# Preparing the next block unit behind the second of seven products, in a fused RWKV-6 attention and SiLU MLP kernel

## The chip, the cores and the metric

The kernel runs on one core of a Trainium2 chip. The metric is the device time of that core in microseconds (us), the median over several runs. A core has five engines with queues of their own, each in order: TensorE (PE in the profile; its weight loads are PEld), VectorE (DVE), ScalarE (ACT), GpSimd (POOL) and SyncE (SP), which here issues nearly all DMAs. Matmuls write to an accumulator memory, PSUM; VectorE and ScalarE read it out.

## The reference

Two stages in float32. First an RWKV-6 attention: for each of 4 batches and 8 heads a 48 x 48 state is carried over 768 tokens.

```python
for t in range(S):
    kt, vt, rt, wt = (k[:, :, t], v[:, :, t], r[:, :, t], w[:, :, t])
    cur = np.einsum('bhd,bhe->bhde', u[None] * kt, vt)
    y[:, :, t] = np.einsum('bhd,bhde->bhe', rt, state + cur)
    state = wt[:, :, :, None] * state + np.einsum('bhd,bhe->bhde', kt, vt)
```

Then the result, as 3072 tokens of 384 channels, goes through an MLP with 2048 hidden channels:

```python
h = x @ w_in
g = h * (1.0 / (1.0 + np.exp(-h)))
return (g @ w_out).astype(np.float32)
```

## The kernel before

**Units.** The tokens are cut into 12 units: six blocks of 128 tokens (`L`) by two pairs of batches. A unit is 256 token columns for the MLP. The first units have a special treatment; from unit 4 (`NPAIR`) on a unit is a "block unit", whose bonus terms (the part with u, and the products inside blocks of 8 tokens) are computed on GpSimd and VectorE.

**Attention of a unit.** The loaded r, k and w (`raw`) are transposed on VectorE (L374) to channels by tokens: `tr`, `tk`, `tw`. `product` (L422) multiplies neighbouring columns of the decays w on GpSimd, level by level, so that level l holds products over 2^l tokens. `grow_keys` (L645) and `grow_own` (L654) multiply the keys with these products on GpSimd; `grow_queries` (L627) does it to the queries on VectorE. `burst` (L704) makes the scores of two levels on TensorE, and `keep_level` (L722) puts them in the score matrix under a mask. `block_bonus` (L507) makes elementwise products of r, k and w in eight steps on GpSimd; `block_sum` (L541) adds them up on VectorE into `block_sums`, which goes out to memory and back by `block_move` (L560, L563). Step 4 of `block_bonus` overwrites `ruk`, which step 0 of `block_sum` reads. At the end of a unit `y_state` (L844) and `y_values` (L852) give the output, ScalarE copies it to `yt` (L857), `update` (L879, L884, L893) makes the new state, and `move_x` (L915) issues ten DMAs on SP that lay `yt` out as `xt`, the input of the MLP. `xt` has a single buffer.

**MLP of a unit.** `up` (L987) makes two of 16 tiles of hidden channels, ScalarE applies SiLU (L996), and `sums` (L1035) forms sums of quarters on VectorE. The second matrix product is done in Strassen's manner by seven smaller products: `quarter` (L1053), each 16 matmul instructions into one of two buffers `p_o` in PSUM. What stands in the buffer is drained by additions on VectorE (L1062); the first product is drained by a copy on ScalarE (L1060). Two products complete the output of a batch, and issue its DMA on SP (L1066). In the order of issue products 2, 3 and 4 read the sums (`own`, `temps` in the profile's names).

**Order.** The schedule is written by hand: each engine carries out its instructions in the order in which the program issues them, and waits on semaphores where data or a buffer is needed. The loop over the units from 3 on interleaves the attention of unit i, cut into groups by `mix(i)`, with the steps of the MLP: the seven products of unit i - 2, then the eight `up` steps of unit i - 1. `room` says how many of these steps follow each group; for a block unit it begins with 3, behind an empty group. The last group of `mix(i)` is the third entry of `end`. It ends with the steps that prepare unit i + 1 and with `move_x(i)`.

**Loads.** `loads` is the list of DMAs for r of the next unit and w and k of the next but one, with the values of the next in their middle. It is dealt out over the groups in `behind`, to the end of each group. The last share thus stands behind `move_x(i)` in SP's queue. Each `load_blocks` step is four DMAs (L123).

Of the kernel before, what the change touches and what calls it, by code (L numbers as in the profile page):

```python
# [38 lines left out]
def kernel(  # L39
# [26 lines left out]
    units = [(n, b0) for n in range(S // L) for b0 in range(0, B, NB)]  # L66
    NSLOT = 2
    NTOK = 2
    NPAIR = 4
# [221 lines left out]
    room = pt.tile([128, 4, DM // 2], F32, name="partial", bufs=1).rearrange("p x d -> p (x d)")  # L291
# [179 lines left out]
    at = 768  # L471
# [447 lines left out]
    def both(fn, i, *args):  # L919
        return [(fn, i, b, *args) for b in range(NB)]  # L920

    def block_loads(i, names="wkr"):
        return [(load_blocks, i, name, g) for name in names for g in range(4)]

    def mix(i):

        ahead = i + 1 < len(units)

        def at(now, *steps):
            return steps if now else ()  # L930

        def bonus_steps(j, *steps):
            return [(block_bonus, j, x) for x in steps]

        def sum_steps(j, *steps):
            return [(block_sum, j, x) for x in steps]

        def turns(j):
            return [*both(turn, j, "w"), (product, j, 0), *both(turn, j, "k"), *both(turn, j, "r"), (grow_own, j, 0)]

        def start(j):
            return [*[(product, j, l) for l in range(1, NL)], (grow_own, j, 1)]

        end = [[*at(ahead, *bonus_steps(i + 1, 0, 1, 2, 3))],
               [*at(i < len(units) - NB, (turn_apart, i), (turn_k, i)), *at(ahead, *turns(i + 1))],
               [(y_state, i), *both(y_values, i), *both(update, i), *at(ahead, *start(i + 1)),
                *at(ahead, *sum_steps(i + 1, 0, 1), *bonus_steps(i + 1, 4, 5)), (move_x, i)]]
        if i < NPAIR:
            groups = [[*both(turn, i, "w"), (product, i, 0)],
                      [*both(turn, i, "k"), *both(turn, i, "r"), (odd_ones, i)], [(start_levels, i), (prepare_keys, i, 1)],  # L950
                      [(prepare, i, 1), *[(product, i, l) for l in range(1, NL)]],
                      [(burst, i, 1), (keep_level, i, 1)],
                      [(keep_level, i, 2), (go_on, i, 2)],
                      [(prepare, i, 3), (reverse_v, i), (bonus, i, 0)],
                      [(burst, i, 3), (keep_level, i, 3), (bonus_sum, i, 0), (bonus, i, 1), (bonus, i, 2)],
                      [(keep_level, i, 4), (go_on, i, 4), (bonus_sum, i, 1), (load_rk, i + 1), (load_u,)],
                      [(prepare, i, 5), (make_block_mask,), (bonus_spread, i), (bonus_write, i)],
                      [(burst, i, 5), (keep_level, i, 5), (keep_level, i, 6), (go_on, i, 6)], *end]
        else:
            groups = [[], [(odd_keys, i, 2), (grow_keys, i, 2, False), (grow_queries, i, 2), *sum_steps(i, 2)],  # L960
                      [(prepare, i, 3), *bonus_steps(i, 6, 7)],
                      [(burst, i, 3), (keep_level, i, 3), *sum_steps(i, 3, 4), (block_move, i), *at(ahead, (load_rk, i + 1))],
                      [(keep_level, i, 4), (go_on, i, 4)],
                      [(prepare, i, 5), (reverse_v, i)],
                      [(block_spread, i), (block_write, i)],
                      [(burst, i, 5), (keep_level, i, 5), (keep_level, i, 6), (go_on, i, 6)], *end]

        loads = [*at(i >= NPAIR and ahead, *block_loads(i + 1, "r")), *at(i + NSLOT < len(units), *block_loads(i + NSLOT, "wk"))]
        if i + 1 < len(units):
            loads.insert(len(loads) // 2, (load_values, i + 1))  # L970

        behind = groups[10 if i < NPAIR else 4 if i == NPAIR else 1:][:4 if i + NSLOT >= len(units) else None]
        for at, group in enumerate(behind):
            group += loads[at * len(loads) // len(behind):(at + 1) * len(loads) // len(behind)]
        return groups
# [92 lines left out]
    def ups(i):  # L1068

        steps = [[(up, i, m)] for m in range(FC // 2)]  # L1070
        for m in range(FH // 2 - 1):

            steps[FH // 2 + 1 + m].append((sums, i, m))
        steps[-1].append((sums, i, FH // 2 - 1))
        return steps

    def downs(i):
        return [[(quarter, i, x)] for x in range(7)]

    def do(*steps):  # L1080
        for fn, *args in steps:
            fn(*args)
# [69 lines left out]
    for i in range(3, len(units)):  # L1152
        steps = downs(i - 2) + ups(i - 1)
        groups = mix(i)
        if i == NTOK + 1:
            groups[4].insert(1, (weight_sums, 3))
        room = (1, 1, 0, 2, 1, 1, 1, 1, 1, 2, 2, 1, 1, 0) if i < NPAIR else (3, 2, 2, 1, 1, 1, 2, 1, 1, 1, 0)
        for group, count in zip(groups, room):
            do(*group)
            for step in steps[:count]:  # L1160
                do(*step)
            steps = steps[count:]
# [32 lines left out]
```

## Time and profile before

| | us |
|---|---|
| median of 3 runs | 606.24 (606.04 to 606.5) |
| the profiled execution | 607.39 |
| its span, first to last instruction | 605.6 |
| seven products (L1053), TensorE busy | 210.1 |
| up (L987), TensorE busy | 259.0 |
| drains of the products (L1062), VectorE busy | 27.4 |

The granted clock of TensorE is 1.0 throughout. The products' time is the sum of four groups of the profile, which names them by what they read: 88.7 + 87.4 + 30.4 + 3.6. The drains' is 11.8 + 7.9 + 7.7. Most of the kernel is a steady loop: from about 130 us on the same series of stages comes back each 45 to 47 us, once for each unit. In the timelines a row is start, duration, engine, line, operation, what it writes and reads, and how many instructions were merged in it; square brackets name the idle time before it and what ended it. SPq is SP's queue, whose durations are those of issuing a DMA and not of the transfer.

### The profile page before, as it was taken

Reading aid. Unit: us, or ns where it says so; the run is one execution under the profiler, and the core shown is the slowest. Engines: PE = TensorE matmul, PEld = TensorE weight load, DVE = VectorE, ACT = ScalarE, POOL = GpSimd, SP = SyncE. Lnnn points to the kernel's source line nnn. Section 1 sums busy time; section 2 is a strip of 40 time slices with the busy share of each in tenths; the row PEclk is TensorE's granted clock in tenths of the full one; section 3 lists DMA queues with packets and bytes.
Section 4 is the critical chain, followed back from the end, with each engine's and each line's share of the span. In section 5 each row is a group of like instructions: output and inputs, shape, how many; then the busy total and the mean of one; then the engine's idle time right before and its main releaser. Section 6 shows DMA issues by size and latency. Waiting matters only on the chain.

```text
span 605.6 us, 15147 instructions
## 1 busy us (share of the span) xinstructions
PE 593.4 (98%) x5982; PEld 529.5 (87%) x5982; DVE 416.8 (69%) x709; ACT 233.2 (39%) x516; POOL 366.6 (61%) x414
## 2 busy tenths in 40 slices
PE   8999999999998999999999999999999999999997
PEld 7787876799888899888889889889889989989997
DVE  7879779798795695696696687587587587451041
ACT  6788874431520530440351351351252242241110
POOL 6998777357578578378478478478568558500000
PEclk9999999999999999999999999999999999999999
DMA  9966693343532543643642643543553441100000
GB/s 224 312 148 168 124 307 47 56 77 49 127 70 48 106 65 52 137 61 56 130 65 50 130 62 53 121 69 52 115 83 53 98 70 27 36 2 27 28 1 26
DMA packets 203079, 53.44 MB, mean 88 GB/s; under 512 B 186752, under 2 KB 194816, under 8 KB 203008
## 3 DMA queue, kind: packets, MB, share of 16 engines
q1 hardware_dynamic: 201424, 51.88, 42.0%
q8 instruction: 47, 0.77, 0.6%
q10 hardware_dynamic: 1584, 0.59, 0.5%
q14 instruction: 24, 0.20, 0.1%
HBM read 43.21 MB, written 5.24 MB: 80 GB/s over the span
## 4 chain that ended last, share of the span: by engine, by line
PE 75%; DVE 8%; DMA 5%; POOL 3%; ACT 3%; SPq 2%; issue 2%; DVEq 0%; POOLq 0%; ACTq 0%
PE p_h L987 31%; PE p_o L1053 31%; PE p_m L1009 3%; PE p_m L852 2%; PE p_sc L704 2%; DMA tokens_w<-in_w_dram 2%; POOL tk L645 2%; DVE temps L1035 2%; PE p_m L704 1%; SPq L123 1%; PE p_m L844 1%; DVE score L722 1%; DVE tr L627 1%; DMA u_bc<-in_u_dram 1%; DVE p_w L242 1%
## 5 line engine op out<-in xcount | busy, mean ns | idle before, releaser
L987 PE MATMUL p_h<-xt,w_in_sb 128*128 128x256 f32 x1152 | 259.0, 382 | 0.9 <-POOL tk L669 0.7
L987 PEld LDWEIGHTS p_h<-xt,w_in_sb 128*128 128x128 f32 x1152 | 215.8, 190 | 32.1 <-POOL tk L669 0.9
L996 ACT ACTIVATE gt<-p_h 128x512 f32<-128x512 f32 x90 | 53.6, 597 | 189.4 <-PE p_h L987 189.1
L645 POOL TENSOR_TENSOR tk<-tk,tw 128x256 f32<-128x256 f32 x128 | 91.2, 734 | 42.8 <-issue 22.9
L1053 PE MATMUL p_o<-own,temps 128*128 128x192 f32 x528 | 88.7, 327 | 3.8 <-DVE temps L1062 3.8
L1053 PEld LDWEIGHTS p_o<-own,temps 128*128 128x128 f32 x528 | 86.0, 190 | 4.7 <-DVE temps L1062 4.6
L1053 PE MATMUL p_o<-w_out_sb,gt 128*128 128x192 f32 x508 | 87.4, 328 | 0.0
L1053 PEld LDWEIGHTS p_o<-w_out_sb,gt 128*128 128x128 f32 x508 | 82.7, 190 | 0.9 <-issue 0.4
L507 POOL TENSOR_TENSOR ruk<-tokens_rk 128x768 f32<-128x768 f32 (+1 forms) x32 | 51.3, 1613 | 49.6 <-DMA tokens_rk<-in_k_dram 25.5
L1035 DVE TENSOR_TENSOR temps<-gt 128x256 f32<-128x256 f32 x84 | 55.8, 664 | 22.4 <-ACT gt L996 22.4
L627 DVE TENSOR_TENSOR tr<-tr,tw 128x512 f32<-128x512 f32 x61 | 56.4, 925 | 18.2 <-PE p_m L704 14.4
L422 POOL TENSOR_TENSOR tw<-tw 128x256 f32<-128x256 f32 (+6 forms) x83 | 43.1, 519 | 37.1 <-DVE tw L374 33.2
L615 ACT COPY tk<-tk 128x256 f32<-128x256 f32 x52 | 21.0, 404 | 97.0 <-POOL tk L645 70.1
L1062 DVE TENSOR_TENSOR partial<-p_o,partial 128x192 f32<-128x192 f32 x33 | 11.8, 358 | 38.3 <-PE p_o L1053 38.1
L722 DVE COPY_PREDICATED score<-mask,p_sc 128x512 f32<-128x512 int8 x42 | 31.2, 798 | 3.1 <-PE p_sc L704 2.9
L1035 DVE TENSOR_TENSOR temps<-temps,gt 128x256 f32<-128x256 f32 x43 | 32.2, 748 | 1.5
L1053 PE MATMUL p_o<-w_out_sb,temps 128*128 128x192 f32 x176 | 30.4, 326 | 0.0
L1062 DVE TENSOR_TENSOR temps<-p_o,partial 128x192 f32<-128x192 f32 x22 | 7.9, 357 | 32.7 <-PE p_o L1053 23.3
L507 POOL TENSOR_TENSOR spare<-tokens_rk 128x384 f32<-128x384 f32 (+1 forms) x16 | 29.3, 1833 | 0.0
L857 ACT COPY yt<-p_m 48x512 f32<-48x512 f32 x40 | 23.2, 581 | 14.9 <-PE p_m L852 10.1
L1053 PEld LDWEIGHTS p_o<-w_out_sb,temps 128*128 128x128 f32 x176 | 28.9, 190 | 0.0
L704 PEld LDWEIGHTS p_sc<-tr,tk 48*32 48x32 f32 (+1 forms) x1312 | 18.2, 119 | 11.3 <-issue 6.8
(187 smaller groups left out, 840.5 us busy)
## 6 DMA issues: line engine op xcount, KB each, us to landing
w_out_sb<-in_moe_w_in_dram SPq DMA_DIRECT2D x6, 768.0 KB, 7.4
w_out_sb<-in_moe_w_out_dram SPq DMA_DIRECT2D x4, 768.0 KB, 5.8
own<-in_moe_w_out_dram SPq DMA_DIRECT2D x4, 768.0 KB, 6.2
tokens_rk<-in_r_dram SPq DMA_DIRECT2D x8, 384.0 KB, 4.4
tokens_rk<-in_k_dram SPq DMA_DIRECT2D x8, 384.0 KB, 5.4
tokens_w<-in_w_dram SPq DMA_DIRECT2D x8, 384.0 KB, 6.4
xt<-yt SPq DMA_DIRECT2D x60, 48.0 KB, 2.0
raw<-in_w_dram SPq DMA_DIRECT2D x80, 32.0 KB, 2.0
```

Of the source, the lines that this page charges most:

```text
L422: engine.tensor_tensor(out=up, in0=t[:, :, 0::2], in1=t[:, :, 1::2], op=ALU.mult)
L507: mul = lambda out, one, two: nc.gpsimd.tensor_tensor(out=out, in0=one, in1=two, op=ALU.mult)
L615: nc.scalar.copy(out=keys(i, X[(l + 1) % 2] * L + c, [4 * c, blocks], [c, 2], [1, c]), in_=keys(i, NP * L + c, [4 * c, blocks], [NP * L + ...
L627: nc.vector.tensor_tensor(out=odd, in0=odd, in1=tw[i][l][:, :, 0::2][:, :, :, None].to_broadcast([128, Q, L >> (l + 1), c]), op=ALU.mult)
L645: nc.gpsimd.tensor_tensor(out=out, in0=have, in1=odd_products(i, l, b, *blocks), op=ALU.mult)
L704: nc.tensor.matmul(to, lhsT=tk[i][rows, X[l % 2] + p, x * m:(x + 1) * m], rhs=have, start=True, stop=True)
L722: nc.vector.copy_predicated(out=dst, mask=masks[l][:, :, None].to_broadcast([128, NB, NP, ni, c]), data=sc[e].rearrange("p (b q) (i c) -> ...
L857: nc.scalar.copy(out=yt[i][PD * e:PD * e + D, :, b, :], in_=p_yt[i, e][PD * b:PD * b + D])
L987: nc.tensor.matmul(p_h[:, a, :], lhsT=w_in_sb[:, c, f * 128:(f + 1) * 128], rhs=xt[i][:, c, :], start=(c == 0), stop=(c == KC - 1))
L996: nc.scalar.activation(out=gt[i, m], in_=p_h, func=AF.Silu)
L1035: nc.vector.tensor_tensor(out=out, in0=one, in1=two, op=op)
L1053: nc.tensor.matmul(p, lhsT=left(f), rhs=right[:, f, :], start=(f == 0), stop=(f == FH - 1))
```

## The change

`end` loses the steps that prepare the next unit: `start` (products of levels 1 to 6 on GpSimd; `grow_own` of level 1, which is two multiplications of the keys on GpSimd and one of the queries on VectorE), block sums 0 and 1, and bonus steps 4 and 5. They are issued in the next unit's `mix` instead, as a new second group, and `move_x` of the unit before goes with them. `room` begins with 2 and 1 for 3, so that products 0 and 1 are issued ahead of the new group and product 2 behind it. All other groups keep their place among the steps; the indices of `behind` are raised by one, since a group was put in front. The last share of the loads stays at the end of its group, and so is issued ahead of the moved steps.

```diff
         end = [[*at(ahead, *bonus_steps(i + 1, 0, 1, 2, 3))],
                [*at(i < len(units) - NB, (turn_apart, i), (turn_k, i)), *at(ahead, *turns(i + 1))],
-               [(y_state, i), *both(y_values, i), *both(update, i), *at(ahead, *start(i + 1)),
-                *at(ahead, *sum_steps(i + 1, 0, 1), *bonus_steps(i + 1, 4, 5)), (move_x, i)]]
+               [(y_state, i), *both(y_values, i), *both(update, i), *at(not ahead, (move_x, i))]]
...
         else:
-            groups = [[], [(odd_keys, i, 2), (grow_keys, i, 2, False), (grow_queries, i, 2), *sum_steps(i, 2)],
+            groups = [[], [*start(i), *sum_steps(i, 0, 1), *bonus_steps(i, 4, 5), (move_x, i - 1)],
+                      [(odd_keys, i, 2), (grow_keys, i, 2, False), (grow_queries, i, 2), *sum_steps(i, 2)],
                       [(prepare, i, 3), *bonus_steps(i, 6, 7)],
...
-        behind = groups[10 if i < NPAIR else 4 if i == NPAIR else 1:][:4 if i + NSLOT >= len(units) else None]
+        behind = groups[10 if i < NPAIR else 5 if i == NPAIR else 2:][:4 if i + NSLOT >= len(units) else None]
...
-        room = (1, 1, 0, 2, 1, 1, 1, 1, 1, 2, 2, 1, 1, 0) if i < NPAIR else (3, 2, 2, 1, 1, 1, 2, 1, 1, 1, 0)
+        room = (1, 1, 0, 2, 1, 1, 1, 1, 1, 2, 2, 1, 1, 0) if i < NPAIR else (2, 1, 2, 2, 1, 1, 1, 2, 1, 1, 1, 0)
```

## The prediction

> **What bounds the kernel now.** I read the busy line of the page first (busy us, share of the span, instructions), then TensorE's waits, then the timeline of each engine around the two longest of them.
>
> ```profile
> PE 593.4 (98%) x5982; PEld 529.5 (87%) x5982; DVE 416.8 (69%) x709; ACT 233.2 (39%) x516; POOL 366.6 (61%) x414
> ```
>
> TensorE's waits (line, tile, who ended the wait; us in total, times, longest):
>
> ```profile
> PE p_o L1053 <- DVE temps L1062: 3.8, 2, 2.4
> PE p_m L1088 <- POOL ident masks.py:199: 1.4, 1, 1.4
> PE p_sc L704 <- DVE score L722: 0.8, 2, 0.6
> ```
>
> TensorE is busy for 593.4 of 605.6 us, so an edit that adds no matmul and takes none away can gain only from the 12.2 us in which TensorE idles. The waits say where: 3.8 us in two waits of the quarter products (L1053) for VectorE's drain of an earlier product (L1062). All other named waits are below 1.5 us and lie in the first 130 us, ahead of the edited loop.
>
> The first of the two, where unit 4 begins (start, duration, engine):
>
> ```profile
> 178.18 2.76 PE L1053 MATMUL p_o<-own,temps 128*128 128x192 f32 x16
> ...
> 183.33 5.47 PE L1053 MATMUL p_o<-own,temps 128*128 128x192 f32 x32 [2.38 <-DVE temps L1062]
> ...
> 179.64 1.12 DVE L893 TENSOR_TENSOR state<-p_sc,state 48x384 f32<-48x384 f32 x2
> 180.77 0.79 DVE L627 TENSOR_TENSOR tr<-tr,tw 128x512 f32<-128x512 f32 x1
> 181.49 0.94 DVE L541 TENSOR_REDUCE block_sums<-ruk 128x16 f32<-128x768 f32 x1
> 182.35 0.54 DVE L541 TENSOR_REDUCE block_sums<-spare 128x8 f32<-128x384 f32 x1
> 182.92 0.36 DVE L1062 TENSOR_TENSOR temps<-p_o,partial 128x192 f32<-128x192 f32 x1
> ...
> 185.03 1.13 DVE L541 TENSOR_REDUCE block_sums<-ruk 128x4 f32<-128x192 f32 x4 [0.90 <-POOL ruk L507]
> ...
> 182.51 2.49 POOL L507 TENSOR_TENSOR ruk<-tokens_rk 128x384 f32<-128x384 f32 x2 [1.49 <-DVE block_sums L541]
> ```
>
> Number the seven products 0 to 6. There are two p_o buffers: product 3 needs the one that product 1 leaves. Product 1 ended at 178.2, its drain came at 182.92, behind the state update and three instructions that prepare unit 4. TensorE finished product 2 at 183.33 - 2.38 = 180.95 and stood still. The second wait is the same at unit 6: product 3 starts at 277.71 after 1.39 us of waiting. At the six other units (5, 7 to 11) VectorE is earlier: at unit 5 the drain starts at 229.09, before product 2 ends at 229.85, and nothing waits.
>
> **The change part by part.** For the eight units 4 to 11:
>
> TensorE and ScalarE keep their orders. So does GpSimd, since products 0 and 1 issue nothing there. Two queues change.
>
> (a) VectorE: the drain of product 1 now stands ahead of the moved L627 and the two L541.
>
> Unit 4: the state update ends at 180.76, the drain runs 180.77 to 181.13. In the trace TensorE went on 0.05 us after the drain's end (183.28 to 183.33), so product 3 starts at 181.18 and not at 183.33: 2.15 us gained, 0.23 of the stall stays.
>
> What is late next: the moved steps, by the drain's 0.36 us. GpSimd's pair that overwrites ruk (L507) waits for the first L541, so it runs 182.87 to 185.36; the four small L541 wait for that pair and end at 186.16 + 0.36 = 186.52; behind them stands the drain of product 3, from 186.60 (it kept 0.08 of distance) to 186.96, and product 5 needs its buffer: 187.01. TensorE would be there at 181.18 + 5.31 = 186.49 (products 3 and 4 took 183.33 to 188.64). A **new wait** of 0.52 us. Product 5 started at 188.64, so unit 4 brings 188.64 - 187.01 = 1.63 us.
>
> Unit 6: the state update ends at 275.12, the drain by 275.5, product 2 at 277.71 - 1.39 = 276.32: the whole 1.39 us goes. Product 5 is due at 276.32 + 5.31 = 281.63; the drain of product 3 (280.62 before) ends at 281.34. No new wait, with 0.24 us to spare.
>
> Units 5, 7 to 11: no wait to gain. VectorE now waits for the end of product 1 before the moved steps: at unit 5 to about 227.35 (a drain starts some 0.15 after its product: 230.00 after 229.85), so L627 comes at 227.71 instead of 226.94, 0.77 us later. What covers it: the drain of product 2 had 0.55 us of idle before it, and two idles of 2.24 us follow. Cost 0; were the cover gone, 6 x 0.77 = 4.6 us.
>
> (b) A rule against row. In the Trainium skill, "GPSIMD Engine Reference", Specifications, says GpSimd shares its SBUF interfaces with VectorE and meets contention from VectorE instructions with two SBUF inputs. The second L627 (tr and tw) is one. The ruk pair took 2.49 us at units 4 and 6, where that L627 ran inside it, and 1.97 at unit 5, where it ran only at the pair's end; rule and row point the same way. They differ in the sum: by the mean row (L507, 1613 ns for mixed shapes) there is nothing to choose, by the rule the order decides. With 1.97 us the new wait at unit 4 would be nil and the gain 2.15. I take 2.49, because L627 still falls inside the pair at unit 4 (183.6 to 184.3). By the same reading the pair becomes 2.49 at the other six, while the tokens_w product behind it returns from 1.04 (unit 5) to 0.59 (unit 4): GpSimd is 0.77 + 0.52 - 0.45 = 0.84 us late there. At unit 5 its keys for the next burst of scores ended at 236.00 and TensorE came for them at 240.29; then GpSimd itself waited 1.23 us for TensorE. Both hold 0.84 us. Cost 0.
>
> (c) SP: the ten issues of move_x fall behind the last chunk of loads of the next unit but one (12 DMAs for unit 4, 8 for units 5 to 10, none for 11). Unit 5 is the tight one, since SP is behind there:
>
> ```profile
> 228.91 7.40 SPq L915 DMA_DIRECT2D xt<-yt  x10
> ...
> 236.34 4.04 SPq L123 DMA_DIRECT2D raw<-in_k_dram  x8
> ...
> 241.38 4.80 PE L987 MATMUL p_h<-xt,w_in_sb 128*128 128x256 f32 x21
> ```
>
> The moves will start 4.04 us later, at 232.95; at the usual 0.588 us each the last starts at 238.25 and lands 1.9 us (the median) later at 240.2. L987 begins at 241.38 and needs the last three pieces only at its third chunk, four matmuls of about 0.22 us on (60 of them take 13.15 us in the chain of waits): 242.25. Slack 2.1 us. In the trace one of these issues took 1.70 us and a landing 3.6: with both the last would land at 239.36 + 3.6 = 242.96, 0.7 us late. I take 0, being nearer to the median; 0 and 0.7 are the ends. Unit 4: moves start at 180.9, landed by 189, needed at 195.0. Unit 6: started at 277.6, landed by 286, needed at 289.4. The other units have SP earlier still. The loads that now come first are for a unit later and gain nothing.
>
> (d) Does the gain of unit 4 live on to unit 6? VectorE's lateness at unit 6 comes through SP: out of the block sums sent out at 245.40, the tokens, and GpSimd's products on them. SP's work at unit 4 was restarted at 197.71 by a VectorE block sum that follows TensorE's burst, so it moves with TensorE's 1.63 us; I take all of it. If it did not move, VectorE would stay on its old clock at unit 6 while TensorE comes 1.63 us earlier: product 5 would start at 281.39 there (behind the drain that ends at 281.34), where it started at 277.71 + 5.31 = 283.02, and all that is left of both gains is 1.63 us.
>
> Sum: 1.63 + 1.39 = 3.02 us. Against the profiled execution: 607.39 - 3.02 = 604.37 (span 605.6 to 602.6). The median of the runs is 606.24, 1.15 below the profiled one; the same stalls taken from it give **603.2**.
>
> **The rivals.**
>
> - Partial gain: (d) fails, or xt is late at unit 5. With (d) failing 1.63 us is left, 604.6; xt alone 3.02 - 0.7 gives 603.9. For it: SP issues without a gap from 202 to 245 in the trace. Against: the restart at 197.71.
> - No change: the wait is replaced by another of its size. The drain of product 3 waits behind GpSimd's pair, and at unit 6 I leave only 0.24 us; if the pair comes 1.5 us later than I think at both units, both gains go: about 606.2. Against: the pair's release is the L541, delayed by 0.36 only.
> - Slower: GpSimd's 0.84 us at six units and 0.36 at two reach TensorE through the keys, 5.04 + 0.72 us. 606.24 - 3.02 + 5.76 = 608.98, 609.0. It decides from the point where GpSimd's delay passes 1.23 us at the keys behind the burst. For it: GpSimd's wait there could hide a second cause. Against: the keys of the burst itself have 4.29 us.
>
> **How the numbers follow.** Forecast case 0.62 (its own range 602.4 to 604.0, from both stalls gone whole, 3.77 us, to 0.7 lost at xt); partial 0.19; no change 0.11; slower 0.08. A measurement of this kernel tells about 0.2% (1.2 us) from no change. Both first cases lie below 605.0: faster 0.81. The range runs from 606.24 - 3.77 = 602.5, less 0.3, to the partial case's 604.6 and 0.6 more (half of what can't be told apart): 602.2 to 605.2. Left out are the last two cases, 0.19.
>
> **What would show it.** Right: TensorE's row of waits for L1062 falls from 3.8 us to below 1 (0.2 before product 3 and 0.5 before product 5 at unit 4), VectorE shows the drain ahead of L627 at all units, idle before it at unit 5, GpSimd's pair is later by 0.4 to 0.8. Wrong: a wait of L987 for the xt moves at unit 5, a wait of the bursts (L704) for L645, or L1062 still named for more than 1.5 us.

## The result, and the profile after

| | before | after |
|---|---|---|
| median of 6 runs, us | 606.31 (605.15 to 607.14) | 603.01 (602.45 to 604.25) |
| profiled execution, us | 607.39 | 603.03 |
| its span, us | 605.6 | 601.2 |
| TensorE's waits for L1062, us | 3.8 in 2 waits | none |

The ratio of the runs is 0.9954, with a 95% interval of 0.9938 to 0.9970: 1.8 to 3.8 us faster. By the two medians it is 3.3 us, by the two profiles 4.4. TensorE's busy time is what it was, within 0.6 us; the idle time went. Of the runs whose granted clock is on record all had 0.999 or more, but for eight long ones among the experiments' and their comparisons' at 0.996 or 0.997, which stay in the medians, and one at 0.655 (870.07 us, with ScalarE's drain), which is left out.

The page of the kernel after, its busy line, and below it the first rows of TensorE's waits:

```profile
PE 592.8 (99%) x5982; PEld 529.6 (88%) x5982; DVE 414.9 (69%) x709; ACT 232.5 (39%) x516; POOL 365.1 (61%) x414
```

```profile
PE p_m L1088 <- POOL ident masks.py:199: 1.4, 1, 1.4
PE p_sc L704 <- DVE score L722: 0.8, 2, 0.6
PE p_h L987 <- POOL tk L669: 0.7, 1, 0.7
```

The row that led TensorE's waits before is gone, and none has come in its place: L987 does not wait for xt, and L704 does not wait for the keys of L645 in the loop. At the start of unit 4, by the timelines of TensorE, VectorE and GpSimd of the kernel after:

```profile
178.03 7.96 PE L1053 MATMUL p_o<-own,temps 128*128 128x192 f32 x48
...
178.45 1.11 DVE L893 TENSOR_TENSOR state<-p_sc,state 48x384 f32<-48x384 f32 x2
179.59 0.36 DVE L1062 TENSOR_TENSOR temps<-p_o,partial 128x192 f32<-128x192 f32 x1
179.87 0.68 DVE L627 TENSOR_TENSOR tr<-tr,tw 128x512 f32<-128x512 f32 x1
180.47 0.95 DVE L541 TENSOR_REDUCE block_sums<-ruk 128x16 f32<-128x768 f32 x1
...
185.00 0.35 DVE L1062 TENSOR_TENSOR partial<-p_o,partial 128x192 f32<-128x192 f32 x1
...
181.50 2.42 POOL L507 TENSOR_TENSOR ruk<-tokens_rk 128x384 f32<-128x384 f32 x2 [1.67 <-DVE block_sums L541]
```

Products 2, 3 and 4 are one unbroken run of 48 matmuls; before, 16 stood ahead of the wait and 32 behind. The drain of product 1 follows the state update at once. The start of the series of products in successive units is a ruler for all of it. From the chain of waits, before and after, the series of units 5 and 7, and 4 to 6 (start, duration):

```profile
221.97 18.40 PE p_o L1053 x112
...
316.35 18.40 PE p_o L1053 x112
```

```profile
172.79 18.40 PE p_o L1053 x112
219.16 18.40 PE p_o L1053 x112
265.58 18.40 PE p_o L1053 x112
```

After, a unit takes 46.4 us (219.16 - 172.79 = 46.37). Before, by the first matmul of each series in TensorE's timeline, unit 4 took 221.90 - 172.88 = 49.02 and unit 6 316.28 - 268.26 = 48.02: 2.65 and 1.65 more, 4.30 us in all, which is nearly all of the 4.4 us between the spans. Unit 5, without a wait, took 46.36. The 45 to 47 us given above for the steady loop leave these two units out. (The chain names a start some 0.07 us later than the timeline, so the two are not mixed.)

### The profile page after: what moved, and what is told of

Its sections match the earlier page's. It is cut to its first block, busy times and chain, and to the rows that moved or that the text cites. A ratio compares the mean times of both kernels' runs of the same rounds, so it can differ in the third digit from the quotient of the medians.

```text
span 601.2 us, 15147 instructions
## 1 busy us (share of the span) xinstructions
PE 592.8 (99%) x5982; PEld 529.6 (88%) x5982; DVE 414.9 (69%) x709; ACT 232.5 (39%) x516; POOL 365.1 (61%) x414
## 4 chain that ended last, share of the span: by engine, by line
PE 87%; DVE 4%; POOL 3%; ACT 2%; DMA 1%; issue 1%; SPq 1%; DVEq 0%; POOLq 0%; ACTq 0%
PE p_h L987 38%; PE p_o L1053 34%; PE p_m L852 3%; PE p_m L1009 3%; PE p_sc L704 3%; PE p_m L704 2%; PE p_m L844 2%; POOL tk L645 1%; DMA u_bc<-in_u_dram 1%; DVE score L722 1%; PE p_sc L879 1%; POOL w_out_sb L255 1%; PE p_m L820 1%; POOL tw L422 1%; POOL w_in_sb L255 1%
## 5 line engine op out<-in xcount | busy, mean ns | idle before, releaser
L987 PE MATMUL p_h<-xt,w_in_sb 128*128 128x256 f32 x1152 | 258.9, 382 | 0.8 <-POOL tk L669 0.7
L987 PEld LDWEIGHTS p_h<-xt,w_in_sb 128*128 128x128 f32 x1152 | 215.8, 190 | 31.9 <-POOL tk L669 0.9
L645 POOL TENSOR_TENSOR tk<-tk,tw 128x256 f32<-128x256 f32 x128 | 94.2, 757 | 37.3 <-issue 21.4
L1053 PE MATMUL p_o<-own,temps 128*128 128x192 f32 x528 | 88.1, 326 | 0.0
L1053 PE MATMUL p_o<-w_out_sb,gt 128*128 128x192 f32 x508 | 87.4, 328 | 0.0
L1053 PEld LDWEIGHTS p_o<-own,temps 128*128 128x128 f32 x528 | 86.0, 190 | 0.3 <-DVE temps L1062 0.3
L507 POOL TENSOR_TENSOR ruk<-tokens_rk 128x768 f32<-128x768 f32 (+1 forms) x32 | 52.3, 1645 | 53.9 <-DMA tokens_rk<-in_k_dram 21.1
L1053 PEld LDWEIGHTS p_o<-w_out_sb,gt 128*128 128x128 f32 x508 | 82.7, 190 | 0.9 <-issue 0.4
L627 DVE TENSOR_TENSOR tr<-tr,tw 128x512 f32<-128x512 f32 x61 | 54.7, 896 | 16.3 <-PE p_m L704 12.6
L1062 DVE TENSOR_TENSOR temps<-p_o,partial 128x192 f32<-128x192 f32 x22 | 7.9, 358 | 36.1 <-PE p_o L1053 26.8
L1062 DVE TENSOR_TENSOR partial<-p_o,partial 128x192 f32<-128x192 f32 x33 | 11.7, 356 | 28.7 <-PE p_o L1053 28.7
L1035 DVE TENSOR_TENSOR temps<-temps,gt 128x256 f32<-128x256 f32 x43 | 30.4, 706 | 1.5
L1053 PE MATMUL p_o<-w_out_sb,temps 128*128 128x192 f32 x176 | 30.4, 326 | 0.0
L541 DVE TENSOR_REDUCE block_sums<-ruk 128x4 f32<-128x192 f32 (+1 forms) x48 | 24.2, 546 | 7.1 <-POOL ruk L507 7.1
L1053 PEld LDWEIGHTS p_o<-w_out_sb,temps 128*128 128x128 f32 x176 | 28.9, 190 | 0.0
L704 PEld LDWEIGHTS p_sc<-tr,tk 48*32 48x32 f32 (+1 forms) x1312 | 18.2, 119 | 11.1 <-issue 7.4
```

Source lines behind the costliest of these rows:

```text
L507: mul = lambda out, one, two: nc.gpsimd.tensor_tensor(out=out, in0=one, in1=two, op=ALU.mult)
L541: add = lambda out, have: nc.vector.tensor_reduce(out=out, in_=have, axis=mybir.AxisListType.X, op=ALU.add)
L627: nc.vector.tensor_tensor(out=odd, in0=odd, in1=tw[i][l][:, :, 0::2][:, :, :, None].to_broadcast([128, Q, L >> (l + 1), c]), op=ALU.mult)
L645: nc.gpsimd.tensor_tensor(out=out, in0=have, in1=odd_products(i, l, b, *blocks), op=ALU.mult)
L704: nc.tensor.matmul(to, lhsT=tk[i][rows, X[l % 2] + p, x * m:(x + 1) * m], rhs=have, start=True, stop=True)
L987: nc.tensor.matmul(p_h[:, a, :], lhsT=w_in_sb[:, c, f * 128:(f + 1) * 128], rhs=xt[i][:, c, :], start=(c == 0), stop=(c == KC - 1))
```

## The experiments

The theory: the gain comes from VectorE's queue alone, because the drain of product 1 no longer stands behind the steps for the next unit. The rivals: it comes from SP's new order; the order of the moved steps itself brings it; or the two profiles only happened to differ. For each kernel the ratio is taken to runs of the kernel before on the same chip. The first four shared one chip (before: 606.12 us, 19 runs from 604.16 to 607.44), the last four another (606.22, 24 runs). The changed kernel was not run on that second chip, so a comparison of these four with its 603.0 us goes across chips.

**The changed kernel again.** No edit.

> The changed kernel once more, beside the runs it is compared with. Drain theory (product 1's drain no longer stands behind VectorE's steps for the next unit): 603.0 us, TensorE waits under 0.5 us for L1062, the kernel before 606.3 with 2 to 4 us of such waits. If the measured gain was a matter of the two profiles only, the two come within 1 us of each other here.

Measured 603.05 us, ratio 0.9949 (0.9933 to 0.9964), span 601.0, no wait for L1062. The gain repeats.

**SP's order alone.** The moved steps behind product 0:

```diff
-(2, 1, 2, 2, 1, 1, 1, 2, 1, 1, 1, 0)
+(1, 2, 2, 2, 1, 1, 1, 2, 1, 1, 1, 0)
```

> The moved steps stand behind product 0 and not behind product 1: SP's order is that of the changed kernel, VectorE's, ScalarE's and GpSimd's orders are those of the kernel before. Drain theory: no gain, 606.3 us, TensorE's waits for L1062 stay at 2 to 4 us. Rival, the gain comes from SP's new order (loads ahead of the xt moves): 603.0.

Measured 606.28 us, ratio 1.0002 (0.9987 to 1.0016). From TensorE's waits in its profile:

```profile
PE p_o L1053 <- DVE temps L1062: 3.0, 2, 1.6
```

The two waits are back, and the gain is gone with them. Moving the steps is worth nothing if they stop one product short; SP's order is worth nothing that shows (the interval is 0.9 us to either side).

**VectorE's order alone.** `move_x` stays at the end of the unit:

```diff
-*at(not ahead, (move_x, i))]]
+(move_x, i)]]
...
-*bonus_steps(i, 4, 5), (move_x, i - 1)],
+*bonus_steps(i, 4, 5)],
```

> The other half: move_x stays at the end of the unit, so SP's order is that of the kernel before, and VectorE's order is that of the changed kernel. Drain theory: all of the gain, 603.0 us. Rival (SP's order): 606.3.

Measured 603.26 us, ratio 0.9960 (0.9942 to 0.9978), span 600.8, no wait for L1062. All of the gain is in this half.

**No step moved, another engine drains.** The kernel before, with:

```diff
             nc.scalar.copy(out=u1, in_=p)
+        if which == 1:
+            nc.scalar.copy(out=c11, in_=p)
+            p = c11
```

> The kernel before with all its orders but one: product 1 is copied out of PSUM by ScalarE (0.32 us, as product 0 is) into its place in the output tile, and VectorE adds u1 there later, from SBUF, where its drain stood. No step is moved. Drain theory: the buffer is free as soon as ScalarE has copied, so the whole gain comes without the move, 603.0 us, no wait of TensorE for L1062 or L1065 above 0.5 us. Rival (the order of the moved steps as such brings the gain): 606.3.

Measured 603.88 us, the median of six runs, ratio 0.9959 (0.9943 to 0.9975), span 601.0; TensorE waits for neither drain. ScalarE's and VectorE's timelines at unit 4:

```profile
178.08 0.32 ACT L1062 COPY temps<-p_o 128x192 f32<-128x192 f32 x1 [2.28 <-PE p_o L1053]
...
178.08 1.11 DVE L893 TENSOR_TENSOR state<-p_sc,state 48x384 f32<-48x384 f32 x2
179.21 0.80 DVE L627 TENSOR_TENSOR tr<-tr,tw 128x512 f32<-128x512 f32 x1
...
181.25 0.92 DVE L1065 TENSOR_TENSOR temps<-temps,partial 128x192 f32<-128x192 f32 x1
```

ScalarE empties the buffer at 178.40; VectorE's addition stays at its late place (the added lines make it L1065, and L1062 the copy), and TensorE does not wait for it. So it is the release of the buffer that counts, not the place of the moved steps.

**The delay doubled.** Block sum 0 done twice, in the kernel before and in the kernel after (`sum_steps(..., 0, 0, 1)` for `sum_steps(..., 0, 1)`).

> The kernel before with block sum 0 done twice (the second writes the same numbers), 0.86 us more of VectorE ahead of product 1's drain at each of the eight units. Drain theory: units 4 and 6 wait 0.86 us longer each, and at units 5 and 7 to 10 the drain now ends some 0.5 us behind product 2, with about 0.27 us more for the restart (the traces show each wait to cost that much beyond the idle time): 1.7 + 5 x 0.8 + 0.5 for unit 11, in all 610.5 to 612.5 us. Rival (VectorE at 69% busy has room for 7 us more): 606.1 to 606.5.

> The changed kernel with the same block sum 0 done twice. Drain theory: the addition stands behind product 1's drain and no longer delays it; what it delays is the drain of product 3, which has some 0.45 us to spare at units 4 and 6 and 1.75 at unit 5: 603.0 to 604.4 us, and waits for L1062 only at units 4 and 6. If the extra work reached TensorE as in the kernel before: 607 to 609.

In the kernel before it costs 6.0 us: 612.24, ratio 1.0094 (1.0063 to 1.0124). Three of its six runs had a granted clock of 0.997; the other three have a median of 611.08, about 5 us more than before. In the kernel after the time is 604.75, ratio 0.9972 (0.9953 to 0.9992), 0.35 us above the range expected; the profiled execution took 603.94. TensorE's waits of the first, and its timeline at unit 5:

```profile
PE p_o L1053 <- DVE temps L1062: 7.1, 8, 2.7
```

```profile
230.37 5.47 PE L1053 MATMUL p_o<-own,temps 128*128 128x192 f32 x32 [0.51 <-DVE temps L1062]
```

and of the second, at units 4 and 6:

```profile
186.00 2.87 PE L1053 MATMUL p_o<-w_out_sb,gt 128*128 128x192 f32 x16 [0.26 <-DVE partial L1062]
...
279.42 2.87 PE L1053 MATMUL p_o<-w_out_sb,gt 128*128 128x192 f32 x16 [0.33 <-DVE partial L1062]
```

Eight waits where there were two, 0.51 us at unit 5 as worked out: in the kernel before, all eight units stood within 0.9 us of this stall. Unit 6 did not wait 0.86 us longer, as expected, but 1.43 us for 1.39. By then unit 5 had cost TensorE 0.79 us more (47.15 for 46.36), and 1.39 + 0.86 - 0.79 = 1.46; this fits the prediction's part (d), that VectorE's lateness at unit 6 comes through SP from unit 4 and does not follow TensorE through unit 5. In the kernel after, product 3 does not wait; product 5 does, behind the drain of product 3, at units 4 and 6 and nowhere else. This is the new wait that the prediction had put at 0.52 us for the change itself.

**One product further.** The moved steps behind product 2:

```diff
-(2, 1, 2, 2, 1, 1, 1, 2, 1, 1, 1, 0)
+(3, 0, 2, 2, 1, 1, 1, 2, 1, 1, 1, 0)
```

> The moved steps behind product 2, so that its drain too stands ahead of them. If the move is better the further back it goes, or only product 1's drain counts: 603.0 us. By the next wait of the sum: the moved steps come 1.2 us (units 4, 6) to 2.7 us (the others) later, GpSimd's pair on ruk and the four small block sums with them, and the drain of product 3 behind these keeps product 5 waiting 0.8 to 1.1 us and 0.27 for the restart at each of eight units: 611 to 614 us, slower than the kernel before, with waits of L1053 for L1062 (partial).

Measured 610.25 us, ratio 1.0061 (1.0040 to 1.0081): slower than before, by a little less than expected. From its waits, and the timelines of VectorE, GpSimd and TensorE at unit 5:

```profile
PE p_o L1053 <- DVE partial L1062: 5.1, 8, 0.6
```

```profile
228.48 0.68 DVE L627 TENSOR_TENSOR tr<-tr,tw 128x512 f32<-128x512 f32 x1
...
232.55 1.13 DVE L541 TENSOR_REDUCE block_sums<-ruk 128x4 f32<-128x192 f32 x4 [0.89 <-POOL ruk L507]
233.60 0.61 DVE L1062 TENSOR_TENSOR partial<-p_o,partial 128x192 f32<-128x192 f32 x2
...
230.11 2.41 POOL L507 TENSOR_TENSOR ruk<-tokens_rk 128x384 f32<-128x384 f32 x2 [4.71 <-DVE block_sums L541]
...
234.00 2.87 PE L1053 MATMUL p_o<-w_out_sb,gt 128*128 128x192 f32 x16 [0.63 <-DVE partial L1062]
```

VectorE sits idle for 2.17 us until product 2 ends, then the moved steps run, GpSimd's pair after them, the small block sums after that, and the drain of product 3 comes too late for product 5. The same buffer, one turn later, at every unit. A unit takes 267.43 - 220.17 = 47.26 us there, 0.9 more than 46.36; times eight, 7.2 us above 603.0, which is the measured time. Behind product 1 is the best of the three places tried.

**The xt moves later.** `move_x` goes from the new group to the head of the group of `prepare` of level 3.

> The changed kernel with move_x one group later (ahead of prepare of level 3), behind four more loads in SP's queue, some 2.0 us, at units 5 on. If the xt moves had room: 603.0 us. By the trace of the changed kernel the last of them starts at 237.4 at unit 5, lands at 239.3 and is needed at 239.45: hardly any room there, 2 us and more elsewhere. So 1.9 us and 0.3 for the restart at unit 5 alone, 605 us, with a wait of L987 for the DMA of xt.

Measured 604.72 us, ratio 0.9974 (0.9954 to 0.9995). The time is the one expected, the profile does not bear out the expected size:

```profile
PE p_h L987 <- DMA xt<-yt: 0.3, 2, 0.2
```

L987 does wait for xt, but for 0.16 us at unit 5 and not 1.9, and for 0.19 us at unit 6, where 2 us of room had been expected. From TensorE's timeline:

```profile
239.97 6.28 PE L987 MATMUL p_h<-xt,w_in_sb 128*128 128x256 f32 x28 [0.16 <-DMA xt<-yt]
...
286.76 5.42 PE L987 MATMUL p_h<-xt,w_in_sb 128*128 128x256 f32 x24 [0.19 <-DMA xt<-yt]
```

At unit 5 none of the ten issues took over 0.80 us in this execution, where one had taken 1.67 in the trace that the expectation was made from: the last move started at 237.85, only 0.4 us later than in the kernel after, and landed about 2 us later, at 239.8. At unit 6 one issue took 1.51 us. The two units are 46.76 and 46.79 us long, 0.39 and 0.42 more than 46.37; that is nearly all of the 0.9 us by which the span, 602.1 us, is longer than that of the kernel after. So the room is used up at two units. The median is 1.7 us longer, and this one profile does not settle what makes the rest; without the two longest runs, 607.36 and 607.65 (granted clock 0.996 and 0.997), it would be 604.53.

## Why the prediction was right, point by point

The forecast was 603.2 us; the median is 603.01. The mechanism was right, and the terms of the sum did less well than the sum.

- **The two waits** at units 4 and 6 were the bound, and the drain's place was their cause: shown by putting the steps behind product 0 (waits back) and by letting ScalarE drain (waits gone with no step moved).
- **Unit 6, 1.39 us:** the wait went whole. It was worth 1.65 us by the length of the unit; each wait costs TensorE 0.27 us beyond the idle time that its row names, which the sum left out.
- **Unit 4, 2.15 us less a new wait of 0.52:** the sizes failed here. In the profile after, none of the old wait is left and the new one isn't there; unit 4 gained 2.65 us. The profile of before was a late execution: GpSimd got its tokens at 162.19 and VectorE's state update began at 179.64, while in the nine other profiles (after and the eight experiments, alike up to there) these stand at 160.1 to 161.0 and 177.9 to 178.8. The kernel behind product 0, which has VectorE's order of before, waited 1.57 us at unit 4, not 2.38; its state update began at 178.81:

  ```profile
  182.50 3.68 PE L1053 MATMUL p_o<-own,temps 128*128 128x192 f32 x21 [1.57 <-DVE temps L1062]
  ```

  So in a less late execution the old wait is smaller, and in the profile after the new one has 0.48 us of room (drain at 185.35, product 5 at 185.83). That it is real when that room goes is shown by the doubled block sum. It was also made too long: behind the drain, GpSimd's pair came 0.17 us later and not 0.36 (at unit 6, 2.88 us after the state update's start before, 3.05 after), because the moved L627 took 0.68 us there for 0.80 and the drain's row and the next overlap by some 0.09. And the 0.08 us of distance was that from the end of product 3 (186.20, the drain at 186.24); the kernel after starts the drain at 185.00, 0.08 ahead of the end of the last small block sum.
- **The sum** of 3.02 us came out close to the 3.3 us of the medians because errors of its terms cancel, and that is luck. With 1.57 for 2.38 at unit 4 it loses 0.81; without the 0.23 and the 0.52 that it took off it gains 0.75; with 0.27 more for each of the two waits it gains 0.54: 3.50 us. The waits of an execution 1.15 us longer than the median were also taken from the median.
- **The contention** of the second L627 with GpSimd's pair: right. At unit 5 the pair took 1.97 us before and 2.45 after, with that L627 now inside it, and the tokens_w product behind it went from 1.04 to 0.58. The keys for the next burst ended 1.15 us later, counted from the start of the series (15.25 for 14.10), and not 0.84, since their own products took 3.06 us for 2.62; TensorE came for them at 237.48, 3.1 us after their end. GpSimd's own wait for TensorE behind them fell from 1.23 to 0.52 us. The trace agrees with what the Trainium skill states in "GPSIMD Engine Reference" (Specifications). The pair before, and after:

  ```profile
  228.68 1.97 POOL L507 TENSOR_TENSOR ruk<-tokens_rk 128x384 f32<-128x384 f32 x2 [1.49 <-DVE block_sums L541]
  ...
  226.56 2.45 POOL L507 TENSOR_TENSOR ruk<-tokens_rk 128x384 f32<-128x384 f32 x2 [2.19 <-DVE block_sums L541]
  ```

- **xt at unit 5:** no wait, as chosen, but with hardly any room, where I had worked out 2.1 us. In the profile after one issue did take 1.67 us, the last move was issued at 237.4 and landed 2.0 us later, and L987's third chunk began at 239.5. The sum also put the issues 0.588 us apart, which is how long one lasts; from start to start they stand 0.63 apart ((7.40 - 1.70) / 9), 0.4 us over the ten.
- **The gain of unit 4 lives on:** the series of unit 6 begins 2.75 us earlier than before (265.51 for 268.26), and that of unit 7 4.40 (311.88 for 316.28). Nothing is given back. SP's restart came with it, as part (d) took it: 194.90 for 197.71.
- **The slower rival** did not come through the keys: no burst waits for L645. A kernel slower than before lies one product further on, and it is slower through the drain of product 3.
- **The signs:** the drain stands ahead of L627 at all units, with 0.55 us of idle before it at unit 5. GpSimd's pair was to be later by 0.4 to 0.8 us; from the start of the series it is 0.69 later at unit 5 but 0.19 at unit 6.

## What to carry to other kernels

When the busiest engine waits for a buffer, look at what stands in the queue ahead of the instruction that frees it: moving that instruction, or giving it to an idle engine, is worth the wait, and the rest of the move is worth nothing. Place such a release between two limits, and work out the next buffer's release as well: one product too early gave no gain here, one product too late was 4 us slower than no move at all. A wait in a single profile is one draw: the sum should be made from several executions or its scatter named.

## What was not expected of the hardware

A wait costs TensorE more than its row of idle time says. Units with a wait of 2.38, 1.39 and 1.57 us (the last in the kernel behind product 0: 221.06 - 172.86 = 48.20) were 2.65, 1.65 and 1.84 us longer than one without: 0.27 us each. The rows show where the 0.27 us lie. Products that follow each other start 2.60 us apart (188.64 and 191.24) though the row of one is 2.76 us long: in the rows each product begins 0.16 us ahead of the end of the last. A wait is counted from that end, so these 0.16 us are lost and not named. And two products behind a wait take 5.47 us where two others take 2.60 + 2.76 = 5.36; the first matmul behind the wait takes 0.43 us where the median is 0.33. All 22 waits of L1053 for VectorE in the profiles of before and of the experiments, from 0.26 to 2.69 us long, show these same 0.16 and 0.10 us. Why the first matmul takes longer was not tried.

The kernel before also scatters. Its 19 runs on one chip span 3.3 us, and the 12 runs of the kernel behind product 0 3.7; the 6 runs of the changed kernel beside them span 1.2 (602.62 to 603.81), the 6 with ScalarE's drain 2.2. More runs span more by themselves, so how much of this the wait makes is not shown. In the profiles the tokens' landing, which varies by 2 us, comes before VectorE's lateness at unit 4, and a drain that has room does not pass it on; that the landing drives the scatter of the runs is argued from the profiles, not shown run by run.
